# Row loads moved to SyncE's queue, the last group read back in 16-partition pieces, and one inverse step earlier, in a two-layer Fourier-filter and MLP kernel

## The chip, the cores and the metric

The kernel runs on one core of one Trainium2 chip. A core has five engines with a queue each: TensorE (PE, with weight loads shown apart as PEld), VectorE (DVE), ScalarE (ACT), GpSimd (POOL) and SyncE (SP). SP, ACT and POOL can issue DMAs; an issue occupies the queue of the engine that makes it, and the transfer itself goes on beside it. The metric is device time in microseconds (us) of one execution, median of several.

## The reference

The input x is 2048 tokens by 1024 features in bfloat16. Two kinds of layer alternate, each with a layer norm in front and a residual add behind, and the same weights are used twice:

```python
def _A_ref(x, w_r, w_i):
    X = rfft2(x)
    X = X * (w_r + 1j * w_i)
    return irfft2(X, s=(S, D)).astype(bfloat16)

def _B_ref(x, w1, b1, w2):
    h = x @ w1 + b1
    return (h * tanh(softplus(h))) @ w2

x = x + _A_ref(_layernorm(x), A_w_r, A_w_i)
x = x + _B_ref(_layernorm(x), B_w1, B_b1, B_w2)
x = x + _A_ref(_layernorm(x), A_w_r, A_w_i)
x = x + _B_ref(_layernorm(x), B_w1, B_b1, B_w2)
```

So the order is spectral layer, MLP, spectral layer, MLP. The MLP is 1024 to 3584 to 1024.

## The kernel before

The spectral layer (`layer_A(li)`, li 0 and 1) makes its two-dimensional transforms out of matmuls with constant tables. The 2048 tokens are split as 16 times 128 and the 1024 features as 8 times 128, and the work runs in seven steps.

Step 1 (`s1`) transforms along the 16 by 8 part. Its input XR holds one (token row of 16, feature block of 8) pair in each of the 128 partitions, and in each partition 128 by 128 values. TensorE runs 16 column groups j of eight matmuls (L635), and ACT (L641) or DVE (L643) copies each result from PSUM. In the first layer three pairs of PSUM banks rotate, so that group j needs the copy of group j-3. Also in the first layer the layer norm's scale is put into the table: `scaled(j)` multiplies the table for group j (L616 on DVE and POOL, L610 on ACT).

In the first layer XR is read straight from x by 32 DMAs of 128 KB in `prologue`: four quarters q of 32 values each, and eight feature blocks h in each quarter. Group j waits for quarter j // 4. Odd h are on POOL's queue and wait for the token tile 13 to be loaded; even h are on SP's queue. In front of them on SP's queue stand the loads of the token tiles; behind them the table FD of step 2, the table JT, the filters of groups 0 and 1, the tables of the first groups and the constants of later steps. POOL's six products of `scaled` stand behind its 16 row loads.

Steps 2, 3, filter, inverse 1 and inverse 2 run over eight groups g with two halves h, in an order that is written out by hand in `order_A`. Each word is stage, group, half: "530" is stage 5, group 3, half 0. Stage 2 (`s2`, L742) transforms along features, stage 3 (`s3`, L787 to L790) along tokens, followed by the product with the filter on DVE (L798 to L805); stage 4 (`i1`, L816) is the first inverse step, whose result ACT copies into V (L827, two buffers, V[g % 2]); stage 5 (`i2`, L841 and L873) is the second inverse step, whose result ACT copies into U (L885, for 31 and 51 DVE at L883; for group 7 in pieces at L574 and L578). PSUM pairs rotate over four here, so each step needs the copies of the step four before it. In the first layer `filter_bins(g)` (L1005, L1016, L1020) and `keep_filter` build and store the filter between these steps.

After step 5 the data are turned through memory. `u_turn` stores U of group g to `u_scratch` on SP's queue, and then reads the group before it back into UT (`u_back`): 16 partitions, 128 columns, 512 KB. For group 7 each half is stored by ACT's queue (256 KB), and `u_last` reads it back: half 0 in two pieces of 8 partitions and 64 columns, half 1 in four pieces of 8 partitions and 32 columns, on SP and ACT. UT has a mark for each quarter of 32 columns. `i4` (L1044) is the last inverse transform: four blocks of 32 columns for the first four token tiles, each needing its quarter of UT from all groups. In between TensorE is kept running by matmuls that change nothing (`spin` L652, `hold` L657) and puts the residual into PSUM (L1033). The first weights of the MLP are loaded by SP after all of UT is in.

A helper (`dma`, L251) issues all these transfers, each engine works through its instructions in program order, and a wait holds up what stands behind it on the same engine.

The order before:

```python
order = ("200 201 210 211 300 301 220 310 400 221 311 401 230 320 410 500 231 321 411 501 330 331 420 510 240 511 421 241 "
         "250 251 340 341 520 350 430 260 521 431 440 261 351 441 530 531 360 361 270 450 451 271 540 541 550 551 460 370 "
         "461 371 560 561 470 471 570 571")
```

Of the kernel before, what the change touches and what calls it, by code (L numbers as in the profile page):

```python
# [7 lines left out]
P = 128  # L8
# [172 lines left out]
class KB:  # L181
# [200 lines left out]
    def prologue(self):  # L382
        sp = self.sp
        self.op(self.pool, lambda e: e.memset(self.EPS[:], 1e-5), writes=[self.r_eps, self.r_warm])
        xt = self.x[0].rearrange("(t p) d -> p t d", p=P)

        for a, b in ((10, 11), (0, 1), (1, 2), (11, 12), (2, 3), (3, 4), (12, 13), (4, 6), (13, 14), (6, 8), (14, 15), (8, 10), (15, 16)):
            self.dma(self.act if a == 10 else sp, self.XS[:, a:b, :], xt[:, a:b, :], f"x{a}", writes=self.r_xs[a:b])
        self.warm(ACT.Sqrt)
        small = {}  # L390
        def load_small(name, n, d):
            b = self.alloc(name, self.o[name], [n], d)
            self.dma(sp, b.ap, self.con[name], name.lower(), writes=[b.res])
            small[name] = b
        load_small("M0", P, BF)
        load_small("IDF", P, F32)
        self.M0, self.IDF = small["M0"], small["IDF"]

        self.XR = self.alloc("XR", self.o["XR"], [P, P])
        self.r_xr = []  # L400
        xv = self.x[0].rearrange("(n2 n1) (h l) -> h n2 n1 l", n2=16, l=P)
        for q in range(4):
            r = Res(f"xr{q}")
            for h in range(8):
                prog = self.pool if h % 2 else sp
                self.dma(prog, self.XR.ap[h:P:8, 32 * q:32 * q + 32, :], xv[h][:, 32 * q:32 * q + 32, :], f"xr{q}{prog.name}",
                         parts=[r], reads=[self.r_xs[13]] if prog is self.pool else [])
            self.r_xr.append(r)
        self.dma(sp, self.FD[:], self.con["FD"], "fd", writes=[self.r_fd])
        load_small("JT", 4 * P, BF)  # L410
        self.JT, self.r_jt = small["JT"].ap, small["JT"].res
        self.w1_next = 0
# [276 lines left out]
    def load_tabs(self, g, sp=False):  # L689
        b = self.FTr[g % 3]  # L690
        self.dma(self.sp if sp else self.pool, b.ap, self.con["FT"][g], f"ft{g % 3}{sp}", writes=[b.res])

    def load_btabs(self, g, sp=False):
        b = self.BTr[g % 3]
        self.dma(self.sp if sp else self.pool, b.ap, self.con["BT"][g], f"bt{g % 3}{sp}", writes=[b.res])
# [9 lines left out]
    def load_w(self, g, after=()):  # L705
        if self.li == 0:
            self.load_wr(self.wr(g), g)
            return
        i = 2 * g % 8
        self.dma(self.pool, self.wt_pair(i), self.w_d[g], f"wt{g % 4}", reads=[self.r_wd[g]] + list(after), writes=[w.res for w in self.WT[i:i + 2]])  # L710

    def layer_A(self, li):
# [7 lines left out]
        dve, act, sp, pool = self.dve, self.act, self.sp, self.pool  # L720
# [5 lines left out]
        def filter_bins(g):  # L726
            ps, banks, _ = self.pair()
            self.filter_bins(g, ps, banks, self.wr(g), WT[2 * g % 8:2 * g % 8 + 2], o["WT"] + 2048 * (2 * g % 8),
                             self.JT, self.r_jt, dve)
# [51 lines left out]
        def s3(g, i):  # L781

            ps, banks, _ = self.pair()
            z, ft = zslot(g, i), FT[g % 3]
            t = ft.ap[:, i, :]
            fns = [
                lambda e: e.matmul(ps[:, 0:512], t[:, 0:128], z.ap[:, 0, :], start=True, stop=False),  # L787
                lambda e: e.matmul(ps[:, 512:1024], t[:, 0:128], z.ap[:, 1, :], start=True, stop=False),
                lambda e: e.matmul(ps[:, 512:1024], t[:, 128:256], z.ap[:, 0, :], start=False, stop=True),
                lambda e: e.matmul(ps[:, 0:512], t[:, 256:384], z.ap[:, 1, :], start=False, stop=True),  # L790
            ]
            self.group(fns, reads=[z.res, ft.res], writes=banks)
            x = X[(2 * g + i) % 4]
            self.op(act, lambda e: e.activation(x.ap.rearrange("p a b -> p (a b)"), ps, ACT.Copy, scale=SIG),  # L794
                    reads=banks, writes=[x.res])
            wt, yk = WT[(2 * g + i) % 8], YK[(2 * g + i) % 6]
            ta, tb = T[2 * i], T[2 * i + 1]
            self.op(dve, lambda e: e.tensor_tensor(ta.ap, x.ap, wt.ap[:, 0:1, :].to_broadcast([P, 2, 512]), ALU.mult),  # L798
                    reads=[x.res, wt.res], writes=[ta.res])
            self.op(dve, lambda e: e.tensor_tensor(tb.ap, x.ap, wt.ap[:, 1:2, :].to_broadcast([P, 2, 512]), ALU.mult),  # L800
                    reads=[x.res, wt.res], writes=[tb.res])
            yk.res.begin()
            self.op(dve, lambda e: e.tensor_tensor(yk.ap[:, 0, :], ta.ap[:, 0, :], tb.ap[:, 1, :], ALU.subtract),
                    reads=[ta.res, tb.res], parts=[yk.res])
            self.op(dve, lambda e: e.tensor_tensor(yk.ap[:, 1, :], tb.ap[:, 0, :], ta.ap[:, 1, :], ALU.add),  # L805
                    reads=[ta.res, tb.res], parts=[yk.res])

        def i1(g, i):

            ps, banks, _ = self.pair()  # L810
            yk, bt, v = YK[(2 * g + i) % 6], BT[g % 3], V[g % 2]
            t = bt.ap[:, i, :]
            fns = []
            for c in range(4):
                for part in range(2):
                    fns.append(lambda e, c=c, part=part: e.matmul(  # L816
                        ps[:, c * 256:(c + 1) * 256], yk.ap[:, part, c * P:(c + 1) * P], t[:, (128, 0)[part]:(384, 256)[part]],
                        start=(part == 0), stop=(part == 1)))
            self.group(fns, reads=[yk.res, bt.res], writes=banks)
            if i == 0:  # L820
                v.res.begin()
            src = ps.rearrange("p (c n) -> p c n", n=P)
            if g == 7:
                for b, prog in enumerate((dve, act)):
                    self.copy(prog, v.ap[:, 4 * b:4 * b + 4, i, :], src[:, 4 * b:4 * b + 4, :], [banks[b]], [], parts=[v.res])
                return
            self.op(act, lambda e: e.activation(v.ap[:, :, i, :], src, ACT.Copy), reads=banks, parts=[v.res])  # L827
# [88 lines left out]

        def u_last():

            def back(prog, half, q, n):
                l = slice(32 * q, 32 * q + 32 * n)  # L920
                self.dma(prog, self.UT.ap[7 + 64 * half:P if half else 64:8, l, :], self.u_d[7][l, 8 * half:8 * half + 8, :].rearrange("l r n -> r l n"),
                         f"ul{half}{q}", reads=[self.r_ud7[half]], parts=self.r_ut[q:q + n])
            back(sp, 0, 0, 2)
            back(sp, 0, 2, 2)
            for q in range(4):
                back((act, sp)[q % 2], 1, q, 1)

        self.s1(li)
        if li:
# [10 lines left out]
        if li == 0:  # L940
            self.WX = [self.alloc(f"WX{i}", o["UT"] + 4096 * i, [2, 2, 512]) for i in range(2)]
            for g in (2, 3, 4):
                load_w(g)
        for stage, g, h in self.order_A():
            if stage == 2:
                s2(g, h)
                if li == 0 and h == (g < 2):
                    filter_bins(g)
                    if g in (0, 1):
                        load_w(g + 5)  # L950
                    elif g == 4:
                        load_w(7)
            elif stage == 3:
                s3(g, h)
                if h:
                    if 1 <= g < 6:
                        load_tabs(g + 2)
                    if li == 0:
                        self.keep_filter(g)
                    elif g < 4:  # L960
                        load_w(g + 4)
            elif stage == 4:
                i1(g, h)
                if h and g < 6:
                    load_btabs(g + 2)
            else:
                i2(g, h)
                u_turn(g, h)
# [7 lines left out]
            self.load_w1(self.w1_buf[fg].ap, fg, [self.w1_buf[fg].res], after=self.r_ut)  # L976

    @staticmethod
    def order_A():


        order = ("200 201 210 211 300 301 220 310 400 221 311 401 230 320 410 500 231 321 411 501 330 331 420 510 240 511 421 241 "
                 "250 251 340 341 520 350 430 260 521 431 440 261 351 441 530 531 360 361 270 450 451 271 540 541 550 551 460 370 "
                 "461 371 560 561 470 471 570 571")
        return [tuple(map(int, w)) for w in order.split()]

    def load_wr(self, wr, g):
# [798 lines left out]
```

## Time and the profile before

| what | us |
|---|---|
| median of 4 runs | 929.86 (927.29 to 932.69) |
| profiled execution, its own time | 929.67 |
| its span, first to last instruction | 927.9 |
| TensorE busy | 875.7 (94%) |
| DVE busy | 622.8 (67%) |
| ACT busy | 435.5 (47%) |
| POOL busy | 158.8 (17%) |
| step 1 of the first layer, TensorE | 22.76 to 37.54 |
| steps 2 to 5 of the first layer, TensorE | 38.70 to 102.88 |
| last store of the first layer issued, first block of `i4` begun | 103.67, 112.45 |
| last store of the second layer issued, first block of `i4` begun | 553.54, 560.92 |

The granted TensorE clock was 0.998 over the span. A timeline row gives start, duration, engine, line, operation, output and input tile, shapes, how many instructions were merged, and in brackets how long the engine had been idle and what ended this. A "q" behind an engine's name is its queue, which issues or waits. In the chain of waits each row is start, duration and what the time was spent on; the chain is followed back from the last instruction to what released it.

### The profile page before, as it was taken

The numbers are of one execution on the slowest core, as the hardware profiler recorded it, in microseconds if no ns is written. First come the engines' busy times: TensorE is split into PE (matmuls) and PEld (weight loads), VectorE is DVE, ScalarE is ACT, GpSimd is POOL, SyncE is SP. The second block draws the span as 40 slices with busy tenths as digits, with TensorE's granted clock in tenths as the row PEclk, the third lists the DMA queues.
The fourth block names the chain that finished last, engine by engine and source line by source line (L and its number), as shares of the span: only waits on it lengthen the run. The fifth ranks groups of instructions, "written<-read, shape, count | busy, mean of one in ns | idle before, by whom it ended". The sixth has DMA issues, their size and how long they took to land.

```text
span 927.9 us, 13536 instructions
## 1 busy us (share of the span) xinstructions
PE 875.7 (94%) x5426; PEld 472.0 (51%) x5503; DVE 622.8 (67%) x987; ACT 435.5 (47%) x643; POOL 158.8 (17%) x186
## 2 busy tenths in 40 slices
PE   0899889999999999999998988999999999999998
PEld 0677576444444444444456766754444444444443
DVE  7798368686789667568767755666747655554473
ACT  7898485456103485420018865757550015552000
POOL 5732003960004651010121200000000000000000
PEclk9999999999999999999999999999999999999999
DMA  9979872674787388364723885445166635732432
GB/s 289 274 244 285 203 197 67 212 274 117 281 271 246 131 321 294 119 239 141 275 90 118 225 212 142 149 160 171 47 196 188 201 133 189 276 120 83 173 122 110
DMA packets 145919, 175.99 MB, mean 190 GB/s; under 512 B 66904, under 2 KB 124472, under 8 KB 145736
## 3 DMA queue, kind: packets, MB, share of 16 engines
q1 hardware_dynamic: 132960, 128.49, 44.5%
q0 software_dynamic: 10800, 45.00, 13.5%
q10 hardware_dynamic: 2096, 1.64, 0.6%
q8 instruction: 43, 0.70, 0.3%
q14 instruction: 20, 0.16, 0.1%
HBM read 130.78 MB, written 40.89 MB: 185 GB/s over the span
## 4 chain that ended last, share of the span: by engine, by line
PE 83%; DVE 6%; DMA 4%; ACT 4%; SPq 2%; issue 1%; ACTq 0%; DVEq 0%
PE PS L1332 36%; PE PS L1233 29%; PE PS L1193 6%; PE PS L816 2%; PE PS L742 2%; SPq L251 2%; PE PS L841 2%; PE PS L1044 2%; DMA ARENA<-in_A_x_dram 1%; DMA ARENA<-u_scratch 1%; PE PS L1154 1%; DVE ARENA L798 1%; ACT ARENA L641 1%; DMA u_scratch<-ARENA 1%; ACT ARENA L452 1%
## 5 line engine op out<-in xcount | busy, mean ns | idle before, releaser
L1332 PE MATMUL PS<-ARENA 128*128 128x512 bf16 x1535 | 338.4, 379 | 1.8
L1233 PE MATMUL PS<-ARENA 128*128 128x512 f16 (+1 forms) x1265 | 279.0, 379 | 2.0 <-DVE ARENA L1238 0.8
L1332 PEld LDWEIGHTS PS<-ARENA 128*128 128x128 bf16 x1568 | 153.2, 98 | 185.0 <-DMA ARENA<-in_B_w_dram 0.5
L1238 DVE TENSOR_TENSOR ARENA<-PS,ARENA 128x512 f32<-128x512 f32 x230 | 157.0, 691 | 100.6 <-PE PS L1233 92.7
L1233 PEld LDWEIGHTS PS<-ARENA 128*128 128x128 bf16 x1288 | 125.4, 98 | 153.2 <-DVE ARENA L1238 3.5
L1243 ACT ACTIVATE ARENA<-ARENA,B 128x512 bf16<-128x512 f32 x138 | 99.0, 722 | 69.0 <-DVE ARENA L1238 63.7
L574 ACT ACTIVATE ARENA<-PS 128x512 f32<-128x512 f32 (+3 forms) x86 | 61.7, 727 | 110.9 <-PE PS L1233 92.5
L1126 POOL TENSOR_TENSOR ARENA<-ARENA 128x512 bf16<-128x512 bf16 x56 | 71.2, 1272 | 75.6 <-DVE ARENA L523 62.0
L452 ACT ACTIVATE ARENA<-XS 128x1024 bf16<-128x1024 bf16 x60 | 63.2, 1054 | 36.2 <-DVE XS L1383 33.0
L1193 PE MATMUL PS<-ARENA 128*128 128x256 bf16 (+1 forms) x524 | 74.7, 299 | 3.6 <-DVE ARENA L1159 1.9
L1357 DVE TENSOR_TENSOR ARENA<-ARENA 128x3584 bf16<-128x3584 bf16 x32 | 63.9, 2018 | 0.0
L1193 PEld LDWEIGHTS PS<-ARENA 128*128 128x128 bf16 x528 | 51.0, 99 | 22.9 <-DVE ARENA L1159 3.3
L1383 DVE TENSOR_TENSOR XS<-PS,ARENA 128x512 bf16<-128x512 f32 x52 | 35.7, 690 | 38.5 <-PE PS L1332 38.2
L1375 DVE TENSOR_TENSOR ARENA<-PS,ARENA 128x512 f32<-128x512 f32 x48 | 32.9, 688 | 27.4 <-PE PS L1332 27.0
L1197 ACT ACTIVATE ARENA<-PS,B 128x256 bf16<-128x256 f32 (+1 forms) x66 | 33.3, 516 | 30.2 <-PE PS L1193 30.0
L1243 ACT ACTIVATE ARENA<-PS,B 128x512 bf16<-128x512 f32 x46 | 31.6, 686 | 18.3 <-PE PS L1233 18.3
L1371 DVE TENSOR_TENSOR ARENA<-ARENA,XS 128x512 f32<-128x512 f32 x52 | 36.8, 732 | 0.6
L443 ACT ACTIVATE RS<-MV,EPS 128x1 f32<-128x1 f32 (+2 forms) x11 | 3.3, 297 | 71.8 <-DVE MV L565 70.1
L794 ACT ACTIVATE ARENA<-PS 128x1024 bf16<-128x1024 f32 x32 | 32.5, 1047 | 5.0 <-PE PS L790 5.0
L816 PE MATMUL PS<-ARENA 128*128 128x256 bf16 x256 | 32.6, 273 | 1.2 <-DVE ARENA L805 1.2
L742 PE MATMUL PS<-FD,ARENA 128*128 128x256 bf16 (+1 forms) x256 | 31.4, 271 | 2.5 <-ACT ARENA L641 1.3
L1208 DVE TENSOR_TENSOR ARENA<-ARENA 128x2048 f16<-128x2048 bf16 x16 | 25.3, 1582 | 9.0 <-PE PS L1193 8.7
(100 smaller groups left out, 816.0 us busy)
## 6 DMA issues: line engine op xcount, KB each, us to landing
ARENA<-in_B_w_dram SPq DMA_DIRECT2D x30, 896.0 KB, 6.8
ARENA<-w1s_scratch SPq DMA_DIRECT2D x28, 896.0 KB, 4.6
ARENA<-w2s_scratch SPq DMA_DIRECT2D x24, 896.0 KB, 6.4
w1s_scratch<-ARENA POOLq DMA_DIRECT2D x14, 896.0 KB, 4.7
ARENA<-in_B_w_dram SPq DMA_DIRECT2D x24, 512.0 KB, 4.3
u_scratch<-ARENA SPq DMA_DIRECT2D x14, 512.0 KB, 5.0
ARENA<-u_scratch SPq DMA_DIRECT2D x14, 512.0 KB, 6.1
w2s_scratch<-ARENA POOLq DMA_DIRECT2D x8, 896.0 KB, 4.1
```

The lines of the kernel that those rows point to most:

```text
L452: self.op(act, lambda e, i=i, f=f: e.activation(junk.ap, x, f, accum_out=sums[:, i:i + 1]), reads=[self.r_xs[j]], writes=[junk.res], parts ...
L574: fn = (lambda e: e.activation(dst, src, ACT.Copy)) if scale is None else \
L742: fns.append(lambda e: e.matmul(dst, at(r), FD[:, t:t + n], start=start, stop=stop))
L816: fns.append(lambda e, c=c, part=part: e.matmul(ps[:, c * 256:(c + 1) * 256], yk.ap[:, part, c * P:(c + 1) * P], t[:, (128, 0)[part]:(384, ...
L1126: self.op(self.pool, lambda e, dst=A(dst), x=A(x), y=A(y), op=op: e.tensor_tensor(dst, x, y, op), reads=[b.res] + list(after), writes=[b.rs])
L1193: fns.append(lambda e, db=db, bank=bank, fl=fl: e.matmul(PS[:, bank, 0:w], wb.ap[:, db, fl * P:(fl + 1) * P], x.ap[:, db, tok], start=(db ...
L1233: self.group([lambda e, db=db: e.matmul(PS[:, bank, :], A[:, db, :], mov[:, db, :], start=(start and db == 0), stop=(db == 3), skip_group_ ...
L1238: self.op(dve, lambda e: e.tensor_tensor(dst.ap, PS[:, bank, :], x.ap, ALU.add), reads=[self.r_bank[bank], x.res], writes=[dst.res])
L1243: self.op(act, lambda e: e.activation(at, src, ACT.Mish, bias=self.B1[:, ft:ft + 1]), reads=[res, self.r_b1], writes=[ra])
L1332: self.group([lambda e, i=i, k=k, b=PB[n][k].ap: e.matmul(PS[:, bank, :], ap[:, i, t * P:(t + 1) * P], b[:, i - 7 * k, :], start=(start an ...
L1357: self.op(dve, lambda e: e.tensor_tensor(ap[dst][:, f, :], ap[x][:, f, :], ap[y][:, f, :], op), reads=part(x, k) + part(y, k), writes=part ...
L1371: self.op(dve, lambda e: e.tensor_tensor(a[t], a[t], x, ALU.add), reads=[rx], writes=[r[t]])
```

## The change

There are three parts. In `prologue` only the odd blocks of quarter 1 stay on POOL's queue, and they now wait for all of quarter 0 to be in; all other row loads are on SP's queue, 28 of them. In `u_last` the six pieces become four, each of 16 partitions and 32 columns; the first two are on ACT's queue and the last two on SP's, and each waits for both halves of the store. In `order_A`, which now gets the layer's number, the steps 540 and 541 stand behind 531 in the first layer; the second layer keeps the order.

```diff
@@ prologue
             r = Res(f"xr{q}")
             for h in range(8):
-                prog = self.pool if h % 2 else sp
+                prog = self.pool if q == 1 and h % 2 else sp
                 self.dma(prog, self.XR.ap[h:P:8, 32 * q:32 * q + 32, :], xv[h][:, 32 * q:32 * q + 32, :], f"xr{q}{prog.name}",
-                         parts=[r], reads=[self.r_xs[13]] if prog is self.pool else [])
+                         parts=[r], reads=self.r_xr[:1] if prog is self.pool else [])
@@ u_last
-            def back(prog, half, q, n):
-                l = slice(32 * q, 32 * q + 32 * n)
-                self.dma(prog, self.UT.ap[7 + 64 * half:P if half else 64:8, l, :], self.u_d[7][l, 8 * half:8 * half + 8, :].rearrange("l r n -> r l n"),
-                         f"ul{half}{q}", reads=[self.r_ud7[half]], parts=self.r_ut[q:q + n])
-            back(sp, 0, 0, 2)
-            back(sp, 0, 2, 2)
             for q in range(4):
-                back((act, sp)[q % 2], 1, q, 1)
+                l = slice(32 * q, 32 * q + 32)
+                self.dma((act, act, sp, sp)[q], self.UT.ap[7:P:8, l, :], self.u_d[7][l, :, :].rearrange("l r n -> r l n"),
+                         f"ul{q}", reads=self.r_ud7, parts=self.r_ut[q:q + 1])
@@ order_A
-        for stage, g, h in self.order_A():
+        for stage, g, h in self.order_A(li):
...
+        if li == 0:
+            order = order.replace(" 540 541", "").replace("530 531", "530 531 540 541")
```

More of the change, by code (lines that the diff above doesn't have):

```diff
@@ L978, in order_A @@
     @staticmethod
-    def order_A():
+    def order_A(li):
         order = ("200 201 210 211 300 301 220 310 400 221 311 401 230 320 410 500 231 321 411 501 330 331 420 510 240 511 421 241 "
```

## The prediction

> **What bounds the kernel now.** I read the chain of work that ended last first, then the timeline of each place that the diff touches, then the DMA rates there. The page's chain says:
>
> ```profile
> PE 83%; DVE 6%; DMA 4%; ACT 4%; SPq 2%; issue 1%; ACTq 0%; DVEq 0%
> ```
>
> Five sixths of the end are TensorE itself, which the change leaves alone. What can move is the rest, at three places: the first transform's input (0 to 39 us), the end of the first spectral layer (80 to 117), and the end of the second (540 to 566). The chain, cut to the start:
>
> ```profile
> 16.60 11.31 DMA ARENA<-in_A_x_dram
> 27.91 0.05 issue
> 27.95 2.75 PE PS L635 x24
> ...
> 38.01 0.69 issue
> ```
>
> TensorE waits for a row load that SP issued at 16.60 and that landed 11.31 us later. The timeline of TensorE shows what that wait is and what follows:
>
> ```profile
> 24.03 2.74 PE L635 MATMUL PS<-ARENA 128*128 128x128 bf16 x24 [0.26 <-ACT ARENA L610]
> 27.95 4.48 PE L635 MATMUL PS<-ARENA 128*128 128x128 bf16 x48 [1.18 <-DMA ARENA<-in_A_x_dram]
> 34.65 1.76 PE L635 MATMUL PS<-ARENA 128*128 128x128 bf16 x24 [0.39 <-ACT ARENA L641]
> 36.92 0.62 PE L635 MATMUL PS<-ARENA 128*128 128x128 bf16 x8 [0.51 <-DVE ARENA L616]
> ```
>
> Four column groups are done at 26.77; the fifth needs quarter 1 of the rows, 1.18 us late. Quarters 2 and 3 are waited for nowhere: the row at 34.65 is group 12, the first of quarter 3, and waits for a copy. Two timeline rows of SP's queue show three row loads each, with POOL's loads in flight and without:
>
> ```profile
> 20.15 7.01 SPq L251 DMA_DIRECT2D ARENA<-in_A_x_dram  x3
> ...
> 27.88 1.97 SPq L251 DMA_DIRECT2D ARENA<-in_A_x_dram  x3
> ```
>
> Beside POOL an issue takes 2.34 us, alone 0.66; the DMA view of 27.3 to 29.8 gives 3.1 us from issue to landing there. The layer ends, from the chain (first layer, then second):
>
> ```profile
> 103.67 4.22 DMA u_scratch<-ARENA
> 107.92 4.30 DMA ARENA<-u_scratch
> 552.48 3.00 DMA u_scratch<-ARENA
> 557.68 5.03 DMA ARENA<-u_scratch
> ```
>
> The last group's store and its read-back stand bare on the path. The DMA view of 552 to 563, 40 slices of 0.275 us, tells why the read-back is slow, and TensorE's rows what it costs:
>
> ```profile
> GB/s 266 259 277 383 465 417 343 410 350 417 380 90 45 7 0 130 263 288 290 290 289 223 177 107 105 125 128 125 140 143 143 145 145 142 134 139 180 22 0 0
> ```
>
> ```profile
> 560.92 0.95 PE L1044 MATMUL PS<-MT,ARENA 128*128 128x32 bf16 x32 [0.54 <-DMA ARENA<-u_scratch]
> 562.75 3.00 PE L1044 MATMUL PS<-MT,ARENA 128*128 128x32 bf16 x106 [0.44 <-DMA ARENA<-u_scratch]
> ```
>
> Group 6's read-back (16 partitions) runs at about 290 GB/s until 558.5; the six pieces of group 7 (8 partitions each) then run at 105 to 145, half of that, until 562.2. TensorE starts the first 32 columns at 560.92 and waits again for the second 32.
>
> **Part 1, the rows.** Twelve of POOL's sixteen issues go to SP, which now has 28. SP's first three issues end at 11.26 and the fourth is held until 14.35 by the token loads ahead of it, as before. From there 24 issues at 0.67 (0.63 and 0.04 between, the chain's pieces at 14.38) end at 30.4. POOL's four now wait for all of quarter 0: eight loads of 128 KB, the eighth issued by 17.0, landing some 2.4 us after its issue's end, about 19.4 (estimate). Behind this wait stand POOL's six products of line 616. Four issues of 0.63 end at 21.9 instead of 21.12; the products start at about 22.0 instead of 21.58. The first two would be done at 23.9 and 25.8 instead of 23.47 and 25.32, and TensorE takes them at 24.9 and 26.7: that cover hides it. Without it the 0.4 would show.
>
> Quarter 1's POOL half, at 4 to 5 us from issue to landing (the uncrowded filter load of 66.88 landed at 71.95), is there at 25.5 to 26.5, ahead of 26.77: the wait of 1.18 goes. Of that, 0.8 reaches the second step: the copies need ScalarE and VectorE, and following groups 4 to 10 through their three PSUM pairs, VectorE's copy of group 10 starts at 32.6 instead of 33.38. What is late next is quarter 3. POOL's four loads crowd SP's queue: before, sixteen of them took 11.7 us of DMA time in which SP moved seven, so four cost SP at most 1.7 us. SP's last issue then starts between 29.8 and 31.5, and lands 3.1 later, or 4.5 as the last one did (29.22 to 33.73): 32.9 to 36.0. TensorE wants it at 33.3 and had it wanted at 34.65. So part 1 is worth from 0.8 gained to 1.4 lost. I take 0.3 gained, a landing at 34.3, nearer to the row of single issues. FD, JT, filters and tables queue behind and come up to 1.6 later; the tightest, the filter of group 0 (landed 38.01, copied at once by VectorE, which then idles 3.23), has cover of 3 us.
>
> [...]
>
> **Part 2, the read-back.** Six pieces (SP four, ACT two) become four of 16 partitions and 32 columns each: ACT the first two quarters, SP the last two. All wait for both halves of the store, so the 256 KB that could be read early no longer is; SP has nothing else between. In the second layer the store is landed at 556.1 (ACT's pieces are issued at 556.11). Group 6 holds the engines until 558.5 as before. Then 512 KB: at the 16-partition rate of 285 GB/s this takes 1.84 us and all is in at about 560.4, the first quarter about 559.6. At the old half rate it takes 4 us, and nothing is gained. TensorE's second 32 columns start at 560.5 instead of 562.75: 2.2 gained. The ends: 0.5 lost, should ACT's second piece queue behind a first issue of 1.17 us (107.92 to 109.09) and the half rate stay; 2.8 gained, should quarters 0 and 1 overtake group 6. I take 2.2, because the nearest row, group 6 itself, has the same source, piece size and partition count.
>
> The rows leave open whether the eight partitions or the second queue halve the rate. [...]
>
> First layer: from the store's landing (107.89) to the end of the four column blocks (116.25) are 8.36 us. With data 2.2 after the issue, 1.84 for 512 KB and three blocks in 2.58 it is some 6.9: 1.45 gained, ends 0.5 lost and 1.8 gained.
>
> **Part 3, the order.** TensorE's work is the same; 540 and 541 (2.0 us at 87.67) move before 360. But their two copies move up on ScalarE too, ahead of those for 360, 361, 270, the filter and 450, 451:
>
> ```profile
> 86.53 1.99 ACT L827 ACTIVATE ARENA<-PS 128x1024 bf16<-128x1024 f32 x2
> 88.74 3.00 ACT L885 ACTIVATE ARENA<-PS 128x1024 bf16<-128x1024 f32 x3 [0.23 <-PE PS L841]
> ```
>
> The L827 pair fills V for group 5, done at 88.52; 1.97 of work ahead makes it 90.49. Step 550 was covered by 540 and 541 and is reached by TensorE at 89.63 in both orders: it now waits 0.85, and 460, 370 and the tail behind it shift by that. In return group 4's store, and read-back 3 behind it on SP, are issued some 5 us sooner. Before, SP's next issues were held (the store at 93.17 for 2.56 us, that at 99.52 for 1.57), and group 6's read-back ran into the last store, which took 4.22 against 2.55 for its twin at 553.54. Freed, it is between 2.55 and 4.22; group 6's read-back now starts nearer to it, so I take 3.1, the lower middle: 1.1 gained. Net 0.25 gained, ends 0.8 gained and 0.85 lost.
>
> **Sum.** 0.3 + 2.2 + 1.45 + 0.25 = 4.2. Against the profiled execution's own 929.67 (span 927.9 and 1.8 around it) that is 925.5; this execution lies 0.2 under the median of 929.86, so it is 0.47% under the median. Everything behind is TensorE's own work, or loads that start from it, and shifts along.
>
> **Rivals.**
> - *The rate stays halved.* If pieces of 256 B on two queues, not the partitions, make 130 GB/s, part 2 gives nothing: 929.67 - 0.55 = 929.1. For it: the low rate begins when the second queue joins. Against it: two queues ran at 350 to 417 while the stores were written, though in larger pieces.
> - *All at the good ends.* Quarter 3 in time (0.8), the last store in 2.55 (0.8), read-backs 1.8 and 2.8: 6.2, so 923.5. For it: all four ends have a row. Against: they need the same quiet DMA engines.
> - *SP's queue becomes the bound of the start (slower).* If issues cost the 1.36 us that the sixteen averaged before (21.78 in all), the 28th starts at 8.07 + 27 x 1.36 = 44.8 and lands at 47.9. TensorE stands at quarter 3, 13.2 late; less the 3.9 of the other parts, 939.0. It decides from a mean of 1.0 us, where quarter 3 lands at 38.6 and all is eaten up. For it: the 2.34 us issues. Against: those had POOL's sixteen loads beside them, and now there are four.
>
> **How the numbers follow.** Forecast 58%, at 925.5 by itself 923.8 to 927.8; halved rate 18%; good ends 14%; SP 10%. A measurement of this kernel can tell about 0.5% from no change, 925.2 below and 934.5 above. The forecast lies across the lower bound, 31 points under it and 27 over. Faster 31 + 14 = 45%; same 27 + 18 = 45%; slower 10%. The range reaches from under the good ends to over the halved rate, 923.0 to 930.0, and leaves out SP's case and the edges.
>
> **What would show it.** Right: no DMA wait before TensorE's fifth group, and at most a small one at the thirteenth; a flat 280 GB/s to the end of both read-backs; second column block by 560.6; a wait of 0.8 before step 550; a shorter last store in the first layer. Wrong: SP's row loads past 33 us, a wait at the thirteenth group over 1 us, the 130 GB/s shelf still there, or the last store still over 4 us.

## The result, and the profile after

| | before | after |
|---|---|---|
| median, us | 927.99 (924.49 to 932.91, 70 executions) | 930.33 (926.17 to 934.53, 45 executions) |
| ratio, 95% interval | | 1.0021 (1.0013 to 1.0029) |
| profiled execution, its own time | 929.67 | 927.48 |
| granted clock in the profiled execution | 0.998 | 1.000 |

The change costs 0.2%. The profiled execution of the changed kernel is a good one, 2.9 under its median, and the profiled execution before lies 1.7 above its own; so the two traces tell places, not the sum.

TensorE at the start, then SP's queue and the chain of waits there:

```profile
24.13 2.97 PE L635 MATMUL PS<-ARENA 128*128 128x128 bf16 x32 [0.26 <-ACT ARENA L610]
...
33.61 1.51 PE L635 MATMUL PS<-ARENA 128*128 128x128 bf16 x24 [1.21 <-ACT ARENA L641]
```

```profile
13.67 17.68 SPq L251 DMA_DIRECT2D ARENA<-in_A_x_dram  x24
```

```profile
25.20 7.45 ACT ARENA L641 x8
...
33.19 5.92 DMA ARENA<-in_A_w_i_dram
```

The wait for quarter 1 before the fifth group is gone (the second profile of the changed kernel, below, has 0.44 us there). From 25.2 the start hangs on ScalarE's copies, back to back, so no more could be won there. Then TensorE stands 1.21 us before the thirteenth group (group 12). The row names ScalarE, but its copy ended at 32.65; the last row load landed at 33.56, and the group starts 0.05 after it. Behind the rows on SP's queue, the filter of group 0 lands at 39.11 and is waited for too, 0.23 us.

The start of the profile before is not the usual one. In it and in the twelve experiments below that leave the rows where they were, the wait before the fifth group is 0 to 1.33 us, 0.67 on average. The thirteenth group starts at 32.6 to 33.2 in eleven of these thirteen profiles, and at 34.30 and, in the profile before, 34.65 in the other two. In the profile before TensorE was slow for longer: the 48 matmuls from 27.95 took 93 ns each, the 24 from 29.12 in the changed kernel's profile 66. So the changed kernel's 33.61 is earlier than in the profile before, but later than usual.

The ends of the two layers, from the chain (first layer) and from TensorE's rows (second):

```profile
103.29 5.54 DMA u_scratch<-ARENA
...
108.91 3.20 DMA ARENA<-u_scratch
```

```profile
558.39 2.58 PE L657 MATMUL PS<-BD,ARENA 128*128 128x512 bf16 x11
561.00 0.95 PE L1042 MATMUL PS<-MT,ARENA 128*128 128x32 bf16 x32
562.02 0.38 PE L657 MATMUL PS<-BD,ARENA 128*128 128x512 bf16 x1
562.24 2.94 PE L1042 MATMUL PS<-MT,ARENA 128*128 128x32 bf16 x105
```

The bandwidth from 552 to 563, in slices of 0.275 us:

```profile
GB/s 256 251 279 297 417 402 432 358 387 305 104 432 387 67 0 115 274 283 286 292 289 234 197 212 205 209 207 206 209 202 210 161 25 0 0 0 60 0 0 0
```

The last store of the first layer takes 5.54 instead of 4.22, its read-back 3.20 instead of 4.30. In the second layer the shelf of 105 to 145 has become one of 205, not of 285, and from the last group's `i2` to the second column block it is 10.94 us (562.24 - 551.30), where it was 12.04 (562.75 - 550.71).

Part of the difference is in no wait. The record of each execution gives its mean granted clock. With the rows where they were (the kernel before and eight of the experiments below) 232 executions had 0.9984 on average, and 11 of them (5%) 0.995 or less; with the rows on SP's queue 70 executions had 0.9969, and 22 (31%) lay that low: 21 of the changed kernel's 58, and one of 12 with the rows alone.

### The profile page after: what moved, and what is told of

Its sections match the earlier page's. It is cut to its first block, busy times and chain, and to the rows that moved or that the text cites. A ratio compares the mean times of both kernels' runs of the same rounds, so it can differ in the third digit from the quotient of the medians.

```text
span 925.7 us, 13530 instructions
## 1 busy us (share of the span) xinstructions
PE 872.1 (94%) x5425; PEld 469.5 (51%) x5503; DVE 622.7 (67%) x987; ACT 435.3 (47%) x643; POOL 150.1 (16%) x174
## 4 chain that ended last, share of the span: by engine, by line
PE 84%; ACT 6%; DVE 6%; DMA 2%; issue 1%; SPq 0%; ACTq 0%; DVEq 0%
PE PS L1330 36%; PE PS L1231 29%; PE PS L1191 6%; ACT ARENA L452 2%; PE PS L816 2%; PE PS L742 2%; PE PS L841 2%; PE PS L1042 2%; ACT ARENA L641 1%; PE PS L1152 1%; DVE ARENA L798 1%; DVE ARENA L800 1%; DMA ARENA<-in_A_w_i_dram 1%; ACT ARENA L794 1%; PE PS L873 1%
```

## The experiments

Every ratio is to executions of the kernel before on the same chip, taken beside the others; the intervals are of 95%. "Stretch A" is the time from the first matmul of step 2 to the last group's `i2` (the row at 100.84 before), "stretch B" from there to the first block of `i4`, both in the first layer; before, they were 62.14 and 11.61.

**One part at a time.** The edits are the hunks of the change, alone or all together.

> The changed kernel once more, beside the kernel before, for the spread. In the profiled execution the changed kernel was 2.2 us shorter in span than the profile of before (925.7 against 927.9), at a granted clock of 1.0 against 0.998, while the median over all runs is 2.3 us longer. Clock theory: the time of one execution follows its granted clock, each 0.002 of it costing about 1.7 us; executions of both kernels at a clock of 1.0 agree within 1 us or the changed one is shorter, and the changed kernel has more executions at 0.996 and less. Path theory: at a clock of 1.0 the changed kernel is still about 2 us longer, and the share of executions with a lower clock is the same in both.

> Part 1 alone (row loads on SP, four on POOL behind quarter 0). By the profile of the changed kernel step 2 begins 1.5 us sooner (37.2 against 38.7). Path theory: 1.0 to 1.5 us shorter than before. Clock theory, if the start is the place: TensorE is busy in fewer of the microseconds between 31.5 and 37.2, so more executions fall to 0.996 or less, and the median is 1 to 2 us longer than before; if it is not the place, 1.0 to 1.5 us shorter with the same clocks as before.

> Part 2 alone (read-back of the last group in four pieces of 16 partitions). Path theory of the prediction: 3.6 us shorter. By the profile of the changed kernel, only about 0.4 us shorter in each layer. Clock theory, if this is the place: TensorE's stand before the first column block grows beyond the filling matmuls, more executions fall to 0.996 or less, and the median is 1 to 2 us longer.

> Part 3 alone (540 and 541 behind 531 in the first layer). Path theory: TensorE waits 0.7 to 0.85 us before step 550, and 1.0 us in all is lost before the last store; 0.5 to 1.1 us longer than before. Clock theory, if the later or longer store is the place: 2 us or more longer with more executions at 0.996 or less; if not, the path's 0.5 to 1.1.

| | median us | ratio, interval | mean clock |
|---|---|---|---|
| before | 927.38 | | 0.9982 |
| the changed kernel again | 930.18 | 1.0027 (1.0007 to 1.0047) | 0.9961 |
| rows alone | 929.86 | 1.0022 (1.0009 to 1.0036) | 0.9970 |
| read-back alone | 926.20 | 0.9983 (0.9967 to 0.9999) | 0.9983 |
| order alone | 928.83 | 1.0017 (1.0003 to 1.0030) | 0.9987 |

The parts add up (0.22%). The read-back gains, rows and order lose, and by the mean clocks only the rows lower it. The second profile of the changed kernel shows a bad start. TensorE's timeline, and its busy time by stretch (stretch, its length, then busy time and instructions of PE, PEld, DVE, ACT and POOL, the granted clock, the DMA share and GB/s):

```profile
37.05 3.59 PE L635 MATMUL PS<-ARENA 128*128 128x128 bf16 x32 [3.98 <-DMA ARENA<-in_A_x_dram]
```

```profile
22.00:34.00 12.00, 7.93 (x96) 6.51 (x96) 10.52 (x10) 11.14 (x16) 11.90 (x8) 1.00 1.03 212
34.00:47.00 13.00, 8.79 (x62) 7.24 (x63) 3.81 (x5) 5.91 (x8) 5.83 (x9) 0.61 0.99 295
```

The last row load, issued at 31.35, landed at 37.01. TensorE stood for 3.98 us (33.07 to 37.05), and had half the clock from 36.17, still within the stand, to 46.41 by the clock records: three times 3.41 us. The first profile of the changed kernel has a clock of 1.00 in the same stretch. With the rows alone, one such piece of 3.41 us lies at 34.35.

**Late rows or low clock?** Two theories for the rows: quarter 3 comes late and the path is longer (P), or the holes it leaves lower the clock (G). First, four of quarter 3's eight loads go back to POOL, behind its product for group 4:

```diff
+            if not li and j == 0:
+                xv = self.x[0].rearrange("(n2 n1) (h l) -> h n2 n1 l", n2=16, l=P)
+                for h in (1, 3, 5, 7):
+                    self.dma(self.pool, self.XR.ap[h:P:8, 96:P, :], xv[h][:, 96:P, :], "xr3b", parts=[self.r_xr[3]])
```

> The row loads of the change alone, but the odd blocks of quarter 3 are on POOL's queue again, behind its product for group 4; SP has 24 row loads. Theory P, the last quarter comes too late on SP's queue: SP's last row load starts near 28 instead of 30.7, quarter 3 is in by 33, the wait at the thirteenth column group falls from 1.2 to 4.0 us to under 0.5, and the time falls from 1.0022 (rows alone) to 0.999 to 1.000 of the time before. Rival: four more loads on POOL slow SP's issues as much as they spare it, or POOL's later products (the rows' four issues are 2.5 us ahead of those for groups 9 to 11) become the wait; then 1.002 or more.

Measured: 1.0013 (0.9998 to 1.0028), clock 0.9966. The rival was right in part. Quarter 3 still landed at 33.86, and TensorE waited 0.75, 1.24 and 1.24 for POOL's products (L616) behind those loads. It tells nothing of P and G. Then the holes were filled with matmuls into a PSUM bank that nobody reads, on the changed kernel, on the kernel before and on the rows alone:

```diff
+            if not li and j > 8:
+                self.fill(8 if j == 12 else 1)
...
+        if not li:
+            self.fill(4)
...
+    def fill(self, n):
+        mov = self.MN.ap[:, 0:4, :].rearrange("p a b -> p (a b)")
+        self.group([lambda e: e.matmul(self.PS[:, 6, :], self.M0.ap, mov, start=True, stop=True)] * n,
+                   reads=[self.M0.res, self.r_mn[0]], writes=[self.r_bank[6]])
```

> The changed kernel with matmuls that change nothing put into the holes of step 1 of the first layer: one of 512 columns before each of groups 9 to 15, eight before group 12, four behind the last (18, at 0.22 us some 4 us of TensorE work in places where it stands idle). Theory G, the changed kernel loses by the lower granted clock that follows the holes at 30 to 37 us: its mean clock goes from 0.997 to 0.9985, and the time falls by about 1.0 to 1.6 us to 1.000 of the time before. Theory P, it loses because quarter 3 is late on SP's queue: the clock may rise, but the time stays within 0.05% of the changed kernel's 1.0021, and it is longer if the filling ends behind the data.

> The kernel before with matmuls that change nothing in the holes of step 1 of the first layer (one of 512 columns before groups 9 to 15, two before group 12, four behind the last: 12, 2.6 us of TensorE work in idle places). With the rows as before, quarter 3 was in at 30.8 to 33.7 in five profiles; on SP's queue at 33.6 to 37.0 in four. Theory G (the clock is the main cost of the rows on SP): without filling the mean clock is 0.9982 here and 0.997 with the rows on SP, with filling both are at 0.9995 or above; so the kernel before gains less by the filling than the changed one did (0.28%): 0.05 to 0.13%, ratio 0.9987 to 0.9995, and about 927.2. Theory P (late rows on the path): the filling gives nothing here, 1.000 or 0.1% more.

> The row loads of the change alone, with the filling of the changed kernel's run (18 matmuls, eight of them before group 12). Rows alone were 1.0022 at a mean clock of 0.997. Theory G: the clock comes to 0.9995 or above and the ratio to 0.9990 to 1.0005, which leaves at most 0.1% between the two placements of the rows at one clock. Theory P: the last quarter still lands at 33.5 to 35, two to three us after that of the old placement, and the ratio stays at 1.0015 or above.

| | without filling, clock | with filling | clock |
|---|---|---|---|
| changed kernel | 1.0021 (1.0013 to 1.0029), 0.9972 | 0.9993 (0.9983 to 1.0004) | 0.9997 |
| before (2 instead of 8 at group 12) | 1, 0.9983 | 0.9999 (0.9988 to 1.0010) | 0.9985 |
| rows alone | 1.0022 (1.0009 to 1.0036), 0.9970 | 1.0012 (1.0001 to 1.0023) | 0.9983 |

On the changed kernel the filling brings back 0.28%, on the rows alone 0.10% (the two intervals overlap), on the kernel before nothing: the holes that matter are mostly those that the rows made. Not all of them: with the order alone, rows where they were, a piece at half the clock lies at 36.80, and five of the 19 profiles, the kernel before among them, have one that begins between 569 and 576. None of the 24 filled executions with rows on SP is at 0.995 or less. But at the clock of before the rows still cost 0.12%. So G and P both hold. A least-squares fit over 191 executions (the four runs of the first table, these three, the read-back with the order below, and the kernel before beside them; a term for each part, one for the filling on each placement of the rows, and a constant for each chip; standard errors that allow for unequal spread) gives for the rows +2.5 us (standard error 0.5), for the read-back -1.6 (0.4) and for the order +1.4 (0.4). With a term for the clock as well, which comes to 0.75 us for each 0.001, the rows keep +1.1 (0.3), and the other two stay as they are (-1.6 and +1.7, 0.2 each). The 1.1 has its place: in 13 profiles with the old rows the last load landed at 30.8 to 33.7, 31.7 on average; in five with the rows on SP's queue at 33.6 to 37.0, 34.8 on average. What it does to TensorE shows best in the filled profiles, which keep a clock of 1.00 here: step 2 begins at 37.13 to 37.40 with the old rows (three) and at 38.19 and 38.67 with the rows on SP's queue, 1.1 later on average (TensorE still waits 0.36 and 0.57 for a row load before the thirteenth group there).

**The order.**

> The read-back and the order of the change, with the row loads as before. Theory A, the parts add: the read-back alone measured 0.9983 and the order alone 1.0017 of the time before, so 1.000 (about 927.4 us beside 927.4), and in the first layer the stretch from the last i2 group (the row at 100.84 before) to the first block of i4 is about 10.6 us as with the read-back alone. Theory B, the two parts collide: with the order changed, group 6's read-back goes out just ahead of group 7's second store, the store takes over 5 us as in the changed kernel (5.54) and that stretch is 11.9; about 1.0009, 928.2 us. In both, the wait before step 550 is 0.7.

Measured: 1.0000 (0.9984 to 1.0016), as A has it, but the trace shows B: stretch A 62.91, stretch B 12.18 (10.58 with the read-back alone), and the chain

```profile
102.67 5.89 DMA u_scratch<-ARENA
108.63 3.12 DMA ARENA<-u_scratch
```

Group 6's read-back was issued at 101.44, 1.2 us ahead of this store. In six profiles it is 0.6 us or more ahead: in five of them the store takes 5.0 to 5.9, in the sixth (the changed kernel with filling, 1.2 ahead) 4.42. In the thirteen where it comes 0.6 or more behind, the store takes 3.2 to 4.6. So being ahead mostly makes the store long, but not by itself. Three kernels try to win back the loss:

```diff
+            if (g, half) in ((3, 1), (5, 1)) or li == 0 and (g, half) == (4, 0):
                 self.op(dve, ...
```
```diff
-                if half == 0:
-                    u_back(6)
                 self.dma(act, self.u_d[g][:, h, :], ...
+                if half == 0:
+                    u_back(6, [] if li else self.r_ud7[:1])
```

> The read-back and the order of the change (1.000; the stretch from the last i2 group to i4 was 12.18 in its profile, the second store of group 7 took 5.89), with group 6's read-back in the first layer held until the first half of group 7's store is in, so that it is issued behind the second store. Theory B, the read-back ahead of the store is what makes the store long: the store takes 2.5 to 4.2, the stretch 10.6 to 11.0 and the ratio 0.9988 to 0.9993. Rival: group 6 comes in later and the stretch stays at 11.9 or above; ratio 1.000 or more.

> The read-back and the order of the change, with the copy of 540 in the first layer on VectorE (which stood idle for 2.45 us there) instead of ScalarE. In five profiles with the new order TensorE waits 0.74 before step 550 and needs 62.9 to 63.2 us from the first matmul of step 2 to the last group's i2 at the full clock, beside 62.1 with the old order. Theory W: ScalarE's two copies moved up are this wait; with one of them gone it falls to 0.2 or less, the stretch to 62.1 to 62.4, and the time by 0.06 to 0.08% of the read-back with the order (1.000). Rival: the wait stays, because V for group 5 is late for another reason, or step 541 now waits for VectorE.

> As the run before, and group 6's read-back in the first layer held until the first half of group 7's store is in. Theory W and B together (the order's loss of 0.16% is the wait before 550, 0.7 to 0.8 us, and the read-back that runs into the last store, about 1 us): all of it comes back, so the ratio of the read-back alone, 0.9983 (0.998 to 0.999), with 62.1 to 62.4 us from step 2 to the last i2 and 10.6 to 10.9 from there to i4. Rival: another cost of the order remains, 0.9995 or more.

| | ratio, interval | A | last store | B |
|---|---|---|---|---|
| read-back and order | 1.0000 (0.9984 to 1.0016) | 62.91 | 5.89 | 12.18 |
| and group 6 later | 0.9997 (0.9985 to 1.0009) | 62.91 | 4.61 | 10.87 |
| and 540 copied by VectorE | 0.9999 (0.9981 to 1.0017) | 62.92 | 5.67 | 12.10 |
| both | 0.9993 (0.9977 to 1.0009) | 62.91 | 4.08 | 10.96 |

The later read-back gives stretch B 1.1 to 1.3 us back, though the store came out a little longer than expected; the ratios are too wide to tell 0.1%. With the order alone, beside the old read-back, stretch B is 11.41, no longer than the 11.31 to 11.90 of five profiles with the old order; there the traces place only the wait before 550, and the rest of the order's 1.4 stays open. Theory W fell. TensorE and ScalarE with one copy on VectorE:

```profile
85.07 1.91 PE L816 MATMUL PS<-ARENA 128*128 128x256 bf16 x16
86.81 1.04 PE L742 MATMUL PS<-FD,ARENA 128*128 128x256 bf16 x8
88.58 1.48 PE L841 MATMUL PS<-ARENA,BD 128*128 128x256 bf16 x12 [0.74 <-ACT ARENA L827]
```

```profile
83.07 1.94 ACT L794 ACTIVATE ARENA<-PS 128x1024 bf16<-128x1024 f32 x2
84.90 1.03 ACT L777 ACTIVATE ARENA<-PS 128x1024 bf16<-128x1024 f32 x1
85.80 0.90 ACT L1018 ACTIVATE ARENA<-PS 128x384 bf16<-128x384 f32 x2
86.54 1.99 ACT L827 ACTIVATE ARENA<-PS 128x1024 bf16<-128x1024 f32 x2
```

The wait is the same 0.74. ScalarE had time for the moved copies; from step 360 on it needs 5.5 us without a break (83.07 to 88.53) until V for group 5 is done, and TensorE, without 540 and 541 in between, has only 4.8 us of work for that time. The cover is what is missing, not ScalarE's time.

**The read-back.** The edits are to the line that issues the pieces: all four on SP (`self.dma(sp, ...`), two pieces of 64 columns on SP, one of 128.

> The read-back of the change alone, with all four pieces on SP's queue and none on ACT's. With two on each queue the pieces came at 205 GB/s and in the order q2, q0, q3, q1. Theory Q, the second queue costs the rate: on one queue all of it comes at 285 GB/s, as group 6's does, the last piece lands about 1.0 us sooner after the store than with both queues (1.7 to 2.0 us after group 6's, instead of 2.4 to 2.7), and in order, so that the first block is never waited for; time 0.3 to 0.8 us under that of the read-back on two queues (0.9983). Rival R, small pieces run at 205 on any queue: same landing of the last piece, but in order, so 0 to 0.4 us. Rival S, one queue's issues at 0.63 us each are the bound: slower by 0.5 us.

> The read-back in two pieces of 16 partitions and 64 columns on SP's queue, rows and order as before. Four pieces of 32 columns came 0.64 us apart, 205 GB/s, on one queue and on two alike. Theory D, each DMA of this shape costs a fixed time between two (0.64 less 0.46 at 285 GB/s: 0.18 us): a piece of 256 KB takes 1.1 us, both land within 2.2 us after group 6's instead of 2.4 to 2.6, and the bandwidth reads 235. Theory E, the rate is that of these addresses: 205 GB/s as before, 1.28 us each. In both the first block waits for 0.4 to 0.6 us more, and the time is within 0.05% of four pieces on SP's queue (0.9969) or 0.05 to 0.1% above.

> The read-back of group 7 as one DMA of 16 partitions and 128 columns (512 KB) on SP's queue, of the very shape of group 6's. Theory D (the size of a DMA sets the rate): 285 GB/s, landing 1.8 to 1.9 us after group 6's. Theory E (it is group 7's own: its rows in DRAM, or that they were written just before): 205 GB/s, 2.5 us after. The time isn't the question; the first block waits for all of it.

| read-back | ratio, interval | GB/s in the second layer | last piece after group 6's, us |
|---|---|---|---|
| ACT and SP, four pieces | 0.9983 (0.9967 to 0.9999) | 202 to 208 | 2.42 |
| SP, four pieces | 0.9969 (0.9956 to 0.9982) | 199 to 215 | 2.39 |
| SP, two pieces | 0.9991 (0.9976 to 1.0006) | 201 to 208 | 2.38 |
| SP, one piece | one execution, 926.46 us | 204 to 209 | 2.45 |

The bandwidth with one piece, 550 to 561, has the step from 290 to 205 where group 6's 512 KB end and group 7's, in the same shape, begin:

```profile
GB/s 202 289 263 295 418 447 380 380 410 201 380 417 134 7 0 127 272 280 292 287 288 215 204 204 207 205 209 206 205 206 204 158 47 0 0 0 0 0 0 61
```

Part of the distance between two pieces and four is their clock (0.9973 and 0.9985 on average; the three executions of each at 1.000 take 924.4 and 924.1 us). Neither the second queue nor the size of a piece sets 205: Q and D fell, R's result came, and E stands, but why group 7's data are slower than group 6's stays open. That they were written just before does not set them apart: in the changed kernel's profile group 6's store was in at 554.80 and its data flow from about 556, group 7's was in at 556.16 and its data flow from about 558. Whether it matters to be the last in line was not tried. What one queue does give is the order: with two queues the pieces land by turns, SP's first (in the changed kernel's second layer q2 at 560.33, q0 at 560.87, q3 at 561.28, q1 at 561.77), on SP alone q0 was in 1.2 us (first layer) and 0.3 us (second) before TensorE took it, and the first block waits for nothing. By the times alone one queue is not shown to be faster than two; the intervals overlap.

**The best of both.** Rows and order as before, four pieces on SP's queue, the filling (two before group 12), and fewer matmuls ahead of `i4`:

```diff
-        self.hold(11 if li else 16, 7)
+        self.hold(10 if li else 11, 7)
```

> A version from what the runs gave: rows and order as before, the read-back in four pieces on SP's queue alone (0.9969), the filling in step 1 (12 matmuls), and the matmuls that keep TensorE running before i4 cut from 16 to 11 in the first layer and from 11 to 10 in the second, because on one queue the first quarter had landed 1.2 and 0.3 us before TensorE took it. If the terms add: 0.9969, less 0.1% by the clock, less 0.1% by the shorter hold (1.1 us and 0.2): 0.995, about 923.5. Rival: the shorter hold lets the data become the wait, or the holes of the kernel before need no filling; then 0.997.

> The best version once more, for a second profile and more executions (five counted in the first run: 0.9956, 0.9942 to 0.9971, at a mean clock of 0.9992). If it holds: 0.9945 to 0.9968; the second quarter-block start 1.23 us after the first in both layers, and no wait for a DMA before i4.

Measured: 923.27 us, 0.9956 (0.9942 to 0.9971), and again 923.64, 0.9960 (0.9942 to 0.9978). It beats both kernels by 0.4% and more. The shorter `hold` brings stretch B from 10.59 (four pieces on SP) to 9.51, and in the second layer the same stretch from 9.50 to 9.29. In the second profile stretch B is 9.51 too, and the chain has only TensorE there:

```profile
103.12 3.43 PE PS L1038 x8
106.55 2.37 PE PS L666 x11
108.93 0.79 PE PS L1049 x32
```

The filling's share in it isn't shown: on the kernel before it gave nothing.

## Why the prediction was wrong

The forecast was 4.2 us gained, 925.5, counted from a profiled execution 1.7 above the median of the kernel before. The changed kernel takes 930.33, 2.3 more than before, and the parts by the fit (2.5 lost, 1.6 gained, 1.4 lost) add up to that.

- *Part 1, the rows: 0.3 gained was predicted, 2.5 (standard error 0.5) were lost.* The mechanism was named, quarter 3 late on SP's queue, and its landing was sized fairly: taken at 34.3, measured at 33.6 to 37.0. Two things failed. The first is the time at which TensorE wants quarter 3: 34.65, or 33.3 without the first wait, was read from the profile before, whose start is a late one. The usual start of the thirteenth group is 32.6 to 33.2, so the predicted landing itself was a loss of 1.1 to 1.7, not a gain of 0.3; and the wait for quarter 1 that was to go is 0.67 on average, not 1.18. In the changed kernel's profile ScalarE's copy let the group start at 32.65; TensorE stood 1.2 there, 1.3 with the rows alone and 4.0 in the second profile. The second is that the working had no term for the clock: around the thirteenth group it was at half for 3.41 us with the rows alone (from 34.35) and for 10.24 us in the second profile of the changed kernel (36.17 to 46.41), and 31% of the executions had a mean clock of 0.995 or less, where 5% had it before. By the fit that is 1.4 of the 2.5. The cover of 3 us that the filter of group 0 was said to have was gone as well: it landed at 39.11 and TensorE waited 0.23. The rival with SP's queue as the bound took the right place with the wrong lever: the issues did not become longer on average (24 in 17.68 us, 0.74 each), the loads only landed 3.0 us later.
- *Part 2, the read-back: 3.65 predicted, 1.6 (0.4) measured.* That fuller DMAs bring the data sooner was right. The step that failed is that the sum let TensorE start when the data are in, and put at nothing the matmuls of `hold` that stand in front, 16 in the first layer and 11 in the second. Before, in the second layer:

```profile
557.80 2.58 PE L657 MATMUL PS<-BD,ARENA 128*128 128x512 bf16 x11
```

  With four pieces on SP's queue no data are waited for, and the first block begins as soon as `hold` lets it:

```profile
554.64 2.58 PE L657 MATMUL PS<-BD,ARENA 128*128 128x512 bf16 x11
557.05 0.95 PE L1040 MATMUL PS<-MT,ARENA 128*128 128x32 bf16 x32
...
558.29 2.99 PE L1040 MATMUL PS<-MT,ARENA 128*128 128x32 bf16 x106
```

  The last `i2` of that profile's second layer starts at 547.55, so it is 9.50 us to the first block and 10.74 to the second (12.04 before); in the first layer 10.59 to the first block (11.61 before). That leaves 1.3 and 1.0 to gain, 2.3 of the 3.65, at any rate of the DMAs. The second block in the second layer was predicted at 560.5, 9.8 after the `i2` at 550.71; it could not start before 10.7. The first layer's 1.45 came near 1.0 without having seen this limit. The rate was missed as well, 205 instead of 285, and costs something where the first quarter comes behind another: with the read-back alone TensorE still waits 0.66 before the second layer's first block, which begins 10.33 after the `i2`. So group 6 was the wrong row to price from. The pieces of 16 partitions did come faster than those of eight, at about 205 GB/s after beside 105 to 145 before.
- *Part 3, the order: 0.25 gained was predicted, 1.4 (0.4) were lost.* The wait before 550 was predicted at 0.85 and is 0.74, but for another reason: the cover moved away, ScalarE's copies did no harm. The last store was to take 3.1 and took 5.54. The working saw that group 6's read-back would start nearer to it, and took that for a lower-middle case; it now starts ahead of the store. Held behind it, the store takes 4.61 and 4.08 beside 5.89 and 5.67 in the same kernels without this.
- *The signs* that the prediction gave were good ones. Of those for "wrong", three came: a wait of over 1 us at the thirteenth group, row loads past 33 us, a last store over 4 us. But the last store had been over 4 us before too (4.22).

## What to carry to other kernels

Price a late load not only by its wait: here the holes that it left in TensorE's work cost about as much again by the clock (1.4 beside 1.1 us), and only many executions showed this, since a single profile may look clean. Read the time at which an engine wants its data from more than one profile: one start may be a late one. Before counting data that come sooner as time gained, look at what the engine itself still has to do in front of them. When a step is moved forward, ask which wait it had covered where it stood, before asking whom it now delays. And when a queue is relieved, look at what it will issue earlier, and into which transfer that runs.

## What the runs showed of the hardware

- The clock records show half the clock for 3.41 us at a time (570.68 to 574.10 in the profile before), and for three times that, 36.17 to 46.41, in the second profile of the changed kernel, where it began within a stand of 3.98 us. But a piece at 34.35 follows waits of only 0.86 and 1.29 (rows alone), one at 36.80 comes where no wait is over 1.2 (order alone), and the changed kernel's first profile kept 1.00 through a wait of 1.21. So holes made it likelier here (with the rows on SP's queue 22 of 70 executions lay at 0.995 or less, with the filling none of 24), and which hole does it is not shown. One such piece at 570, in the profile before, cost 1.65 us: from the first matmul of the second MLP to the end 357.39 (570.47 to 927.86), and 355.74 in the changed kernel's profile, which has none.
- On one queue and on two, in four pieces, in two and in one, 512 KB of 256 B pieces came back at about 205 GB/s right behind 512 KB of the same shape at about 290 (second layer).
- The last store of 256 KB took 2.0 to 2.6 us in the second layer and 3.2 to 5.9 in the first. There it took 5.0 or more only where a read-back of 512 KB had been issued ahead of it, in five profiles of six.
